# An RWKV-7 recurrence from chunks of 128 tokens to tiles of two 64-token chunks with quarter products

## The chip, the cores and the metric

The kernel runs on one core of a Trainium2 chip. The metric is the device time of one execution in microseconds. The core has TensorE (matmul and, beside it, weight load: PE and PEld in the profile), VectorE (DVE), ScalarE (ACT), GpSimd (POOL) and SyncE (SP), which issues most of the transfers.

## The reference

The first half is a recurrence over 768 tokens for 4 batches of 8 heads with 40 features, in float32. With the state S (40 x 40 for a head) and the token's vectors r, k, v, w, a, b:

```
y_t = r_t S
Sa  = S a_t
S   = S * w_t - Sa b_t^T + v_t k_t^T
```

The outputs y of a token's heads are put together to a row of 320. The second half sends each of the 3072 rows to one of 8 experts by its token id (`id * 2654435761 % 8`) and computes `relu(x @ w1[e]) @ w2[e]`, with w1 of 320 x 1024 and w2 of 1024 x 320.

## The kernel before

The recurrence runs in chunks of 128 tokens of one batch, 24 in all (`chunk`, from line 301). A chunk holds its tokens on the partitions. With P the running product of the decays w inside the chunk, at = a P, bt = b / P and kt = k / P, the chunk needs C from (I + A) C = r1, where A is the strictly lower part of at bt^T (a 128 x 128 block for each head) and r1 comes from the state at the chunk's start and from the values v. From C follow y, and the state after the chunk.

The steps of a chunk stand in this order. VectorE clamps the decays (L312) and takes their least and greatest (L313, L314), TensorE transposes them (L317), VectorE multiplies them up along time with a scan (L321), TensorE turns the result back (L329), VectorE takes the reciprocal (L334), and GpSimd forms at, bt and kt (L335 to L337). `turned` (L264) transposes four 128 x 128 blocks on TensorE and copies the bank on ScalarE. `masked` (L285) multiplies pairs of these for the four heads of one parity and masks the result on VectorE. A head pair lies on partitions 0 to 39 and 64 to 103; `products` (L279) issues four products after each other, all of one parity.

The inverse of I + A is built in seven levels, from blocks of one row to blocks of 64. A level masks A between two blocks on GpSimd (`between`, L351), multiplies it with the inverse so far (x_ps), then again (n_ps), adds on VectorE (L381), and transposes the sum (tm_ps). The last level has 64 x 64 blocks only. After it come r1 (L404 to L408), C (ct_ps, L413), its scores with r (mrc), y (L433 to L438), the state (s_ps, L453 and L454) and its transpose (L463).

Two chunks run at a time, half a chunk apart: each is a generator, and the loop at L471 takes a step of one and a step of the other in turn. That loop stands in a manual schedule: TensorE, VectorE, ScalarE and GpSimd get their instructions in the order in which the program issues them. SyncE's transfers are not bound to it. Each engine runs its own queue in order.

Ahead of the recurrence stands the routing (L122 to L213): each token's place among its expert's slots is counted, and 24 indirect transfers from GpSimd write the token numbers into a list in DRAM (L189), which is read back (L196). The experts' w1 tiles have a pool of their own from the start; the first two experts' w1 are loaded during the recurrence. w2, the gathers of rows (`gather`, L498), `up` (L511) and `down` (L523) follow for expert after expert. At the end a check of the decays decides whether a loop over single tokens runs, and a loop over surplus tiles; neither does in these runs.

Of the kernel before, what the change touches and what calls it, by code (L numbers as in the profile page):

```python
# [36 lines left out]
def kernel(  # L37
# [19 lines left out]
    DP = 64  # L57
    NCH = S // P
    HP = H // 2
    LEVELS = 7  # L60
# [14 lines left out]
    wpool = pool("wpool", 2)  # L75
    ps = pool("ps", 8, space=bass.MemoryType.PSUM)

    def bank(shape, name):
        return ps.tile(shape, F32, tag="ps", name=name)

    # DRAM
# [3 lines left out]
    # masks; s is the partition, t the free index  # L85
# [8 lines left out]
    nupper = const.tile([P, P], F32)  # L94
    nc.vector.tensor_scalar(nupper[:], upper[:], -1.0, None, op0=OP.mult)
    level = []
    for l in range(LEVELS):
        t = const.tile([P, P], F32, name=f"level{l}")
        c2, r2 = (const.tile([P, P], I32, name=f"{n}{l}", tag=n) for n in ("c2", "r2"))
        nc.vector.tensor_scalar(c2[:], col[:], l, None, op0=OP.logical_shift_right)  # L100
        nc.vector.tensor_scalar(r2[:], row[:], l, None, op0=OP.logical_shift_right)
        nc.vector.tensor_tensor(t[:], c2[:], r2[:], op=OP.not_equal)
        nc.vector.tensor_scalar(c2[:], c2[:], 1, None, op0=OP.logical_shift_right)
        nc.vector.tensor_scalar(r2[:], r2[:], 1, None, op0=OP.logical_shift_right)
        e2 = const.tile([P, P], F32, name=f"e2{l}", tag="e2")
        nc.vector.tensor_tensor(e2[:], c2[:], r2[:], op=OP.is_equal)
        nc.vector.tensor_tensor(t[:], t[:], e2[:], op=OP.mult)
        nc.vector.tensor_tensor(t[:], t[:], upper[:], op=OP.mult)
        level.append(t)
# [3 lines left out]
    def over_heads(t):  # L113
        return t[:].unsqueeze(1).to_broadcast([P, HP, P])

    # decays outside LO .. HI are looked for in every chunk
    wmin = route.tile([P, B * NCH], F32)
    wmax = route.tile([P, B * NCH], F32)

# [1 line left out]
    tok_h = dataclasses.replace(moe_token_ids.tensor, shape=list(moe_token_ids.tensor.shape))  # L121
    tok = route.tile([P, TPP, 2], I32)  # L122
    nc.sync.dma_start(tok[:], tok_h.bitcast(I32).rearrange("(p c two) -> p c two", p=P, two=2))
    iota_e = const.tile([P, E], I32)
    nc.gpsimd.iota(iota_e[:], pattern=[[1, E]], base=0, channel_multiplier=0)
    token = const.tile([P, TPP], I32)
    nc.gpsimd.iota(token[:], pattern=[[1, TPP]], base=0, channel_multiplier=TPP)

    eid = route.tile([P, TPP], I32)
    nc.vector.tensor_scalar(eid[:], tok[:, :, 0], E - 1, None, op0=OP.bitwise_and)  # L130
    mine = route.tile([P, E, TPP], F32)
    nc.vector.tensor_tensor(
        mine[:], eid[:].unsqueeze(1).to_broadcast([P, E, TPP]),
        iota_e[:].unsqueeze(2).to_broadcast([P, E, TPP]), op=OP.is_equal)
    mflat = mine[:].rearrange("p e c -> p (e c)")
    tot_ps = bank([P, E * TPP], "tot_ps")
    nc.tensor.matmul(tot_ps[:], lhsT=ones[:], rhs=mflat, start=True, stop=True)
    bef_ps = bank([P, E * TPP], "bef_ps")
    nc.tensor.matmul(bef_ps[:], lhsT=upper[:], rhs=mflat, start=True, stop=True)
    rst = route.tile([P, E, TPP], F32)  # L140
    nc.vector.memset(rst[:], 1.0)
    nc.vector.memset(rst[:, :, 0:1], 0.0)
    cum = route.tile([P, E, TPP], F32)
    cumf = cum[:].rearrange("p e c -> p (e c)")
    nc.vector.tensor_tensor_scan(cumf, rst[:].rearrange("p e c -> p (e c)"), tot_ps[:], 0.0,
                                 op0=OP.mult, op1=OP.add)
    cnt = route.tile([P, E], F32)
# [101 lines left out]
    def flat(t):  # L249
        return t[:].rearrange("p h x -> p (h x)")  # L250
# [424 lines left out]
```

## Time and profile before

| | us |
|---|---|
| median of 3 runs (1681.71 to 1682.19) | 1682.03 |
| span of the profiled execution | 1676.6 |
| TensorE busy | 1510.4 |
| weight loads busy | 1255.9 |
| VectorE busy | 602.3 |
| ScalarE busy | 479.7 |
| GpSimd busy | 534.1 |

The profiled execution is a run of its own; the trace gives its span, from the first to the last instruction, and the time of the runs is a little longer than that span. Busy times are sums over the span and hide that it has stages: a start of some 80 us in which TensorE mostly waits, the recurrence to about 1291 us, and the experts from about 1309 us. A float32 product appears in the trace as two records of a weight load and two of a matmul; a transpose as one of each.

### The profile page before, as it was taken

The page shows a single profiled execution, that of the slowest core. Times are in us where ns is not written, and L with a number is a line of the kernel's source. Part 1 is how long each engine was busy: PE and PEld are TensorE (multiplying, and loading weights), DVE is VectorE, ACT ScalarE, POOL GpSimd, SP SyncE. Part 2 cuts the span into 40 slices and gives each one's busy share as a digit, 9 for nine tenths or more (in the row PEclk, how much of TensorE's full clock was granted, in tenths as well). Part 3 has the DMA queues.
Part 4 walks back from the last instruction along what each step waited for, and adds up shares of the span by engine and source line. Part 5 has one row for each costly group of instructions (what it writes and reads, how often), then busy time and mean ns, then how long its engine had stood idle before and what let it go on. Part 6 is the DMA issues. An engine that isn't in the chain of part 4 may idle for free.

```text
span 1676.6 us, 27809 instructions
## 1 busy us (share of the span) xinstructions
PE 1510.4 (90%) x11622; PEld 1255.9 (75%) x11622; DVE 602.3 (36%) x980; ACT 479.7 (29%) x897; POOL 534.1 (32%) x480
## 2 busy tenths in 40 slices
PE   2399999999999999999999999999997899999996
PEld 1388988988888888888889888899996344444443
DVE  7144444444344444434443444444431111111110
ACT  0143333333333333333333334333331000000000
POOL 5643233443224442234432344423340211111100
PEclk9799999999999999999999999999996799999998
DMA  5111111011101111101111001110001222222200
GB/s 123 13 21 29 29 21 21 17 29 29 29 17 21 21 29 29 23 15 21 29 28 29 17 17 25 29 29 9 5 5 54 79 72 82 91 90 90 83 12 13
DMA packets 172719, 59.58 MB, mean 36 GB/s; under 512 B 156974, under 2 KB 168239, under 8 KB 172592
## 3 DMA queue, kind: packets, MB, share of 16 engines
q1 hardware_dynamic: 168752, 48.58, 13.1%
q0 software_dynamic: 3840, 9.20, 1.7%
q8 instruction: 93, 1.52, 0.4%
q14 instruction: 34, 0.28, 0.1%
HBM read 49.85 MB, written 9.21 MB: 35 GB/s over the span
## 4 chain that ended last, share of the span: by engine, by line
PE 77%; DVE 8%; POOL 6%; issue 5%; DMA 2%; ACT 0%; SPq 0%; POOLq 0%; DVEq 0%; ACTq 0%
PE n_ps L282 13%; PE x_ps L282 13%; PE up_ps L516 12%; PE dn_ps L526 8%; PE tm_ps L268 6%; POOL um L358 4%; PE y_ps L438 3%; PE y_ps L436 2%; PE r_ps L406 2%; PE mrc_ps L282 2%; PE mrv_ps L282 2%; POOL bl L353 2%; DVE um L381 2%; PE ct_ps L413 2%; DVE um L360 2%
## 5 line engine op out<-in xcount | busy, mean ns | idle before, releaser
L353 POOL TENSOR_TENSOR bl<-nat,level 128x512 f32<-128x512 f32 x240 | 309.6, 1318 | 67.3 <-PE x_ps L282 67.3
L282 PE MATMUL n_ps<-um,xm 128*128 128x128 f32 (+1 forms) x2304 | 288.1, 271 | 0.2
L282 PEld LDWEIGHTS n_ps<-um,xm 128*128 128x128 f32 (+1 forms) x2304 | 257.2, 183 | 10.5 <-ACT xm L392 2.4
L282 PE MATMUL x_ps<-tm,bl 128*128 128x128 f32 x1920 | 263.7, 282 | 0.0
L270 ACT COPY tm<-tm_ps 128x512 f32<-128x512 f32 x288 | 169.2, 588 | 329.3 <-PE tm_ps L268 328.1
L381 DVE TENSOR_TENSOR um<-n_ps,um 128x512 f32<-128x512 f32 x240 | 162.8, 687 | 258.3 <-PE n_ps L282 258.3
L282 PEld LDWEIGHTS x_ps<-tm,bl 128*128 128x128 f32 x1920 | 233.5, 193 | 13.8 <-issue 3.9
L268 PE MATMUL tm_ps<-ident,um 128*128 128x128 f32 x1152 | 181.6, 280 | 43.9 <-DVE um L360 26.6
L335 POOL TENSOR_TENSOR at<-al,pr 128x320 f32<-128x320 f32 x24 | 27.9, 1162 | 567.8 <-ACT pr L331 567.8
L516 PE MATMUL up_ps<-xt,w 128*128 128x512 f32 (+1 forms) x384 | 194.5, 637 | 8.7 <-issue 7.5
L374 ACT COPY xm<-x_ps 128x512 f32<-128x512 f32 x240 | 140.7, 586 | 206.1 <-PE x_ps L282 206.1
L268 PEld LDWEIGHTS tm_ps<-ident,um 128*128 128x128 f32 x1152 | 129.8, 143 | 62.1 <-DVE um L381 24.6
L516 PEld LDWEIGHTS up_ps<-xt,w 128*128 128x128 f32 (+1 forms) x384 | 63.4, 191 | 135.5 <-issue 135.5
L526 PE MATMUL dn_ps<-w,ht 128*128 128x320 f32 x512 | 140.0, 434 | 0.0
L526 PEld LDWEIGHTS dn_ps<-w,ht 128*128 128x128 f32 x512 | 96.6, 190 | 45.3 <-issue 6.1
L530 POOL DMA_INDIRECT out_dram<-o,idx_all x32 | 31.7, 990 | 273.0 <-ACT o L529 267.9
L360 DVE TENSOR_TENSOR um<-um,ident 128x512 f32<-128x512 f32 x48 | 82.5, 1718 | 65.0 <-POOL um L358 65.0
L289 DVE TENSOR_TENSOR mrc<-mrc_ps,nupper 128x512 f32<-128x512 f32 x48 | 31.0, 687 | 161.7 <-PE mrc_ps L282 161.7
L358 POOL TENSOR_TENSOR um<-nat,level 128x512 f32<-128x512 f32 x48 | 61.0, 1270 | 80.1 <-DVE nat L289 80.1
L519 DVE TENSOR_SCALAR ht<-up_ps 128x512 f32<-128x512 f32 x32 | 22.2, 692 | 177.4 <-PE up_ps L516 141.5
L438 PE MATMUL y_ps<-bt,mrc 128*128 128x40 f32 x384 | 77.6, 288 | 0.0
L521 ACT ACTIVATE ht<-up_ps 128x512 f32<-128x512 f32 x32 | 19.1, 597 | 199.8 <-PE up_ps L516 199.8
(161 smaller groups left out, 1810.8 us busy)
## 6 DMA issues: line engine op xcount, KB each, us to landing
w<-in_moe_w_dram SPq DMA_DIRECT2D x8, 1280.0 KB, 7.8
w<-in_moe_w_dram SPq DMA_DIRECT2D x8, 1024.0 KB, 5.6
al<-in_a_dram SPq DMA_DIRECT2D x24, 160.0 KB, 2.5
bl<-in_b_dram SPq DMA_DIRECT2D x24, 160.0 KB, 2.6
kl<-in_k_dram SPq DMA_DIRECT2D x24, 160.0 KB, 3.0
w<-in_w_dram SPq DMA_DIRECT2D x24, 160.0 KB, 2.5
v<-in_v_dram SPq DMA_DIRECT2D x24, 160.0 KB, 2.5
r<-in_r_dram SPq DMA_DIRECT2D x24, 160.0 KB, 2.5
```

Source lines behind the costliest of these rows:

```text
L268: nc.tensor.transpose(p[:, hp, :], src, ident[:])
L270: nc.scalar.copy(t[:], p[:])
L282: nc.tensor.matmul(p[out_, hp, cols], lhsT=lhs(hp), rhs=rhs(hp), start=True, stop=True)
L353: nc.gpsimd.tensor_tensor(nxt[par][:], nat[par][:], over_heads(level[l]), op=OP.mult)
L358: nc.gpsimd.tensor_tensor(t[:], nat[par][:], over_heads(level[0]), op=OP.mult)
L360: nc.vector.tensor_tensor(t[:], t[:], over_heads(ident), op=OP.add)
L374: nc.scalar.copy(xm[par][:], x_ps[:])
L381: nc.vector.tensor_tensor(t[:], n_ps[:], um[par][:], op=OP.add)
L406: nc.tensor.matmul(r1_ps[:, h * D:(h + 1) * D], lhsT=mak[par][:, hp, :], rhs=vt[:, h, 0:D], start=first, stop=True, skip_group_check=True)
L438: nc.tensor.matmul(o, lhsT=mrc[par][:, hp, :], rhs=bt[:, h, 0:D], start=False, stop=True, skip_group_check=True)
L516: nc.tensor.matmul(p[:], lhsT=w1[0:m, c, f * P:(f + 1) * P], rhs=xt[0:m, c, 0:n], start=(c == 0), stop=(c == 2))
L526: nc.tensor.matmul(p[:], lhsT=ht[:, f, j * P:(j + 1) * P], rhs=w2[:, f, :], start=(f == 0), stop=(f == FP - 1))
```

## The change

The recurrence is written anew; the experts stay. A tile u is now 64 tokens of two batches, so that the partitions hold 2 x 64 tokens; there are again 24 tiles (12 chunks, two groups of batches). Operands of 40 or 64 partitions are multiplied into 64 output partitions, so that a product takes a quarter of the array: `quarters` walks through the four combinations of head parity (which partitions are read) and batch (which partitions are written), and `scores` writes the two parities to two banks.

The order of all instructions is a plan: each step has a tick and an order, and the sorted plan is issued. A tile has four parts. `tile_a` (at tick u) makes the decay products, at, and b / P (called ba), and sends the blocks of -A that the inverse needs to DRAM. `group_i` inverts the 32-row blocks of four tiles at a time: it reads them from DRAM, one 32 x 32 block on each of the 128 partitions, runs 30 steps of two VectorE instructions, and sends the result back through DRAM. `tile_m` makes the inverse of 64 rows from two blocks of 32. `tile_s` (ten ticks after `tile_a`) loads r, v, k and b again and makes the scores, and `tile_b` makes r1, C, y and the state. The reciprocal of P is kept from `tile_a`.

The check of the decays becomes one comparison of the clamped with the loaded decays. The routing becomes a generator whose steps stand in the plan at ticks 8, 8.5, 9 and so on. The pool of w1 is opened after the recurrence's pools are closed, and the first w1 is loaded there.

The core of the diff:

```diff
-    NCH = S // P
+    C = 64
+    NCH = S // C
+    NG = B // 2
+    NU = NCH * NG
+    BLK = 32
+    GRP = 4
...
-    level = []
...
-    # ---- routing ----
...
+    ps1 = apool("ps1", 2, space=bass.MemoryType.PSUM)
+    ps2 = apool("ps2", 3, space=bass.MemoryType.PSUM)
...
+    HELD = 11
+    LD = 2
...
+    a_dram = [nc.dram_tensor(f"a_blocks{i}", (GRP, 4, H, BLK, BLK), F32) for i in range(NU // GRP)]
+    u_dram = [nc.dram_tensor(f"u_blocks{i}", (GRP, 4, H, BLK, BLK), F32) for i in range(NU // GRP)]
...
+    def quarters(both=True):
+        for hp in range(HP):
+            for p in range(2):
+                for be in range(2):
+                    yield hp, p, be
...
+    def load(dst, src, n, g):
+        for be in range(2):
+            nc.sync.dma_start(
+                dst[half(be), :, 0:D],
+                src[2 * g + be, :, n * C:(n + 1) * C, :].rearrange("h t e -> t h e"))
...
+    def scores(lt, rt, p, co=0):
+        for hp, par, be in quarters():
+            mm(p[half(be), par, co + hp * C:co + (hp + 1) * C],
+               lt[half40(par), hp, half(be)], rt[half40(par), hp, half(be)])
...
+    T1, Q1, T2, Q2, T3, Q3, T4, Q4 = (i / 8 for i in range(8))
...
+    def tile_a(u):
...
+        @at_tick(u - 0.6)
...
+            for nm, src in (("w", w), ("a", a), ("b", b)):
+                x[nm] = work.tile([P, H, D], F32, tag=f"{nm}l", name=f"{nm}l", bufs=LD)
+                load(x[nm], src, n, g)
+        @at_tick(u + T1)
...
+            nc.vector.tensor_scalar(heads(wc), x["w"][:], LO, HI, op0=OP.max, op1=OP.min)
+            p = turn(pairs(wc), "w_ps")
...
+            nc.scalar.copy(dec[:, :, 1:], wt[:, :, 0:C - 1])
...
+        @at_tick(u + T1, 5)
...
+            nc.vector.scalar_tensor_tensor(junk[:], heads(x["wc"]), 0.0, x["w"][:], op0=OP.add,
...
+            nc.vector.tensor_tensor_scan(
...
+            nc.vector.tensor_tensor(pend[:], x["w_ps"][:, :, C - 1], pt[:, :, C - 1], op=OP.mult)
...
+        @at_tick(u + T2, 5)
...
+            nc.gpsimd.tensor_tensor(heads(at), x["a"][:], pr[:], op=OP.mult)
...
+            nc.vector.reciprocal(inv[:], inv[:])
+            nc.gpsimd.tensor_tensor(heads(ba), x["b"][:], inv[:], op=OP.mult)
...
+        @at_tick(u + 1 + Q2, 1)
...
+            scores(x["ba_t"], x["at_t"], p)
...
+            for i in range(2):
+                nc.scalar.mul(na[i][:], pv[:, :, :, i * BLK:(i + 1) * BLK], -1.0)
+            for q in range(4):
+                nc.sync.dma_start(
+                    a_dram[u // GRP][u % GRP, q].rearrange("h s t -> s h t"),
+                    na[q % 2][q * BLK:(q + 1) * BLK].rearrange("s two h t -> s (two h) t"))
+    def group_i(gi):
...
+        t0 = gi * GRP + GRP + 1.0
...
+            nc.sync.dma_start(nb[:], a_dram[gi][:].rearrange("g q h s t -> (g q h) s t"))
...
+            nc.gpsimd.affine_select(ub[:], nb[:], pattern=[[-1, BLK], [1, BLK]], base=0,
...
+        for j in range(1, BLK - 1):
+            @at_tick(t0 + 3.9 * (j - 1) / (BLK - 2), 9)
+            def _(j=j):
+                ub, nb = x["u"], x["n"]
+                m = BLK - 1 - j
+                t = work.tile([P, BLK * BLK // 4], F32, tag="outer", name="outer")
+                tv = t[:, 0:j * m].rearrange("p (c i) -> p c i", c=j)
+                nc.vector.tensor_tensor(tv, ub[:, 0:j, j:j + 1].to_broadcast([P, j, m]),
+                                        nb[:, j, j + 1:].unsqueeze(1).to_broadcast([P, j, m]), op=OP.mult)
+                o = ub[:, 0:j, j + 1:]
+                nc.vector.tensor_tensor(o, o, tv, op=OP.add)
+
...
+            nc.sync.dma_start(u_dram[gi][:].rearrange("g q h s t -> (g q h) s t"), x["u"][:])
+            for i in range(GRP):
+                um = tiles[gi * GRP + i]["um"] = um_r(gi * GRP + i)
+                for q in range(4):
+                    o = (q % 2) * BLK
+                    nc.sync.dma_start(um[q * BLK:(q + 1) * BLK, :, o:o + BLK],
+                                      u_dram[gi][i, q].rearrange("h s t -> s h t"))
...
+    def tile_m(u, t0):
...
+        @at_tick(t0 - 1 + Q4, 2)
...
+            for h in range(H):
+                nc.vector.transpose(t11[:, h, :], um[:, h, 0:BLK])
+            p = bank([P, H, BLK], "x_ps")
+            for hp, par, be in quarters():
+                q = slice(be * C, be * C + BLK)
+                o = slice(be * C + BLK, (be + 1) * C)
+                mm(p[o, hx(par, hp), :], na[q, par, hp, :], t11[q, hx(par, hp), :])
...
+    def tile_s(u, t0):
...
+            for nm, src in (("k", k), ("b2", b)):
+                x[nm] = work.tile([P, H, D], F32, tag=f"{nm}l", name=f"{nm}l", bufs=2)
+                load(x[nm], src, n, g)
...
+        for i, (nm, bufs) in enumerate((("r", 3), ("v", 1), ("kt", 1))):
+            @at_tick(t0 - 1 + (T1, T2, T3)[i], 2)
+            def _(nm=nm, bufs=bufs):
+                x[nm + "_t"] = turned(pairs(x[nm]), nm + "_t", bufs)
...
+            p = two_banks("m_ps")
+            scores(x["kt_t"], x["at_t"], p)
+            scores(x["v_t"], x["r_t"], p, HP * C)
...
+            nc.vector.tensor_tensor(t[:], p[:].rearrange("p two (h t) -> p (two h) t", t=C),
+                                    after[:].unsqueeze(1).to_broadcast([P, 4 * HP, C]), op=OP.mult)
...
+    def from_state(p, lt, s):
...
+    def tile_b(u, t0):
...
+            @at_tick(t0 - 1 + Q4, 1)
...
+                from_state(p, x["at_t"], st)
...
+        @at_tick(t0 + Q1, 0)
...
+            for hp, par, be in straight_then_crossed():
+                mm(p[half(be), par, hp * D:(hp + 1) * D], mak(x, par, hp)[half(be)],
+                   head(x["v"], par, hp)[half(be)], start=first and hp == 0)
...
+            nc.scalar.copy(by_pair(r1), heads_of(p))
...
+        @at_tick(t0 + Q2, 0)
...
+                mm(p[half(par), be, hp * C:(hp + 1) * C], head64(x["r1"], par, hp)[half(be)],
+                   x["um"][half(be), hx(par, hp), :])
...
+            @at_tick(t0 + T3, 0)
...
+                p = turn([ct[:, hp, :, :] for hp in range(HP)], "nc_ps")
...
+        @at_tick(t0 + Q3, 1)
...
+            @at_tick(t0 + Q3, 2)
...
+                for src, rhs, begin in ((x["kt"], x["v"], True), (x["bt"], x["nct"], False)):
+                    for hp, par, be in quarters():
+                        mm(p[half(par), be, hp * D:(hp + 1) * D], head64(src, par, hp)[half(be)],
+                           head(rhs, par, hp)[half(be)], start=begin and hp == 0, stop=not begin)
...
+        @at_tick(t0 + Q4, 3)
...
+                mm(o, mrv(x, par, hp)[half(be)], head(x["kt"], par, hp)[half(be)],
+                   start=first and hp == 0, stop=False)
+                mm(o, x["mrc"][half(be), par, hp, :], head(x["bt"], par, hp)[half(be)], start=False)
...
+            nc.vector.tensor_tensor(by_pair(xs), heads_of(p), by_pair(x["pr"]), op=OP.mult)
...
+            @at_tick(t0 + Q4, 6)
...
+    LAG = 10
+    for u in range(NU):
+        tile_a(u)
+        tile_s(u, u + LAG)
+        tile_m(u, u + LAG)
+        tile_b(u, u + LAG)
+    for gi in range(NU // GRP):
+        group_i(gi)
...
+    steps = routing()
+    for i in range(12 + TPP):
+        at_tick(8 + 0.5 * i, 7)(lambda: next(steps, None))
...
+        for *_, f in sorted(plan, key=lambda e: e[:3]):
+            f()
     a_ctx.close()
+    wpool = pool("wpool", 2)
+    w1s[0] = load_w1(moe_w1[0], "w1_0")
```

## Rows read from the trace of the kernel before

**Rows 1.** Busy time by stretch; columns: us, PE, PEld, DVE, ACT, POOL, PEclk, DMA share, GB/s

```profile
40.00:80.00 40.00, 10.64 (x67) 9.62 (x68) 5.00 (x7) 3.52 (x6) 25.63 (x25) 0.81 0.20 14
...
700.00:1000.00 300.00, 283.16 (x2633) 264.18 (x2632) 131.54 (x189) 111.04 (x209) 109.08 (x90) 1.00 0.13 23
...
1280.00:1320.00 40.00, 26.09 (x83) 16.42 (x83) 6.02 (x17) 0.60 (x1) 9.55 (x10) 0.53 0.37 111
```

**Rows 2.** The chain of waits in order of time; columns: start us, us, what

```profile
56.64 9.13 DMA slot_tokens<-token,key_i
...
1205.79 1.95 PE x_ps L282 x16
...
1253.46 1.95 PE x_ps L282 x16
...
1291.99 6.59 DMA x_rows<-xs
...
1308.86 28.05 PE up_ps L516 x48
```

**Rows 3.** Groups of the inverse on TensorE; columns: line, shapes, count | busy us, mean ns

```profile
L282 PE MATMUL x_ps<-tm,bl 128*128 128x128 f32 x1920 | 263.7, 282 | 0.0
...
L268 PE MATMUL tm_ps<-ident,um 128*128 128x128 f32 x1152 | 181.6, 280 | 43.9 <-DVE um L360 26.6 <-DVE um L381 17.2
```

**Rows 4.** Order of time, weight loads; columns: start us, us, engine, line, shapes, count

```profile
1003.98 0.20 PEld L453 LDWEIGHTS s_ps<-v,kt 128*64 128x64 f32 x4
...
1004.79 0.22 PEld L454 LDWEIGHTS s_ps<-nct,bt 128*64 128x64 f32 x4
...
1012.12 0.47 PEld L268 LDWEIGHTS tm_ps<-ident,um 128*128 128x128 f32 x4
...
1012.55 0.47 PEld L268 LDWEIGHTS v_t_ps<-ident,v 128*128 128x128 f32 x4
...
1034.54 0.97 PEld L282 LDWEIGHTS n_ps<-um,xm 128*128 128x128 f32 x8
...
1035.63 0.54 PEld L282 LDWEIGHTS x_ps<-tm,nat 64*64 64x64 f32 x8
...
1036.24 0.86 PEld L282 LDWEIGHTS n_ps<-um,xm 128*128 128x128 f32 x7
```

**Rows 5.** Order of time, matmuls of the two parities

```profile
62.72 0.27 PE L282 MATMUL mak_ps<-at_t,kt_t 40*128 40x128 f32 x1
...
62.72 0.27 PE L282 MATMUL nat_ps<-at_t,bt_t 40*128 40x128 f32 x1
```

**Rows 6.** Groups by shape on VectorE, ScalarE and GpSimd

```profile
L180 DVE TENSOR_TENSOR slot<-slot,rank 128x24 f32<-128x24 f32 x1 | 0.2, 164 | 0.0
...
L441 DVE TENSOR_TENSOR xs<-y_ps,pr 128x320 f32<-128x320 f32 x24 | 11.8, 492 | 89.5 <-PE y_ps L438 89.5
...
L321 DVE TENSOR_TENSOR_SCAN pt<-dec,restart 128x516 f32<-128x516 f32 x24 | 29.3, 1222 | 0.0
...
L334 DVE RECIPROCAL inv<-inv 128x320 f32<-128x320 f32 x24 | 51.7, 2153 | 0.8
...
L360 DVE TENSOR_TENSOR um<-um,ident 128x512 f32<-128x512 f32 x48 | 82.5, 1718 | 65.0 <-POOL um L358 65.0
...
L130 DVE TENSOR_SCALAR eid<-tok 128x24 int32<-128x24 int32 x1 | 9.4, 9382 | 1.1 <-DMA tok<-in_moe_token_ids_dram 1.1
...
L270 ACT COPY tm<-tm_ps 128x512 f32<-128x512 f32 x288 | 169.2, 588 | 329.3 <-PE tm_ps L268 328.1 <-ACT r_t L270 0.2
...
L335 POOL TENSOR_TENSOR at<-al,pr 128x320 f32<-128x320 f32 x24 | 27.9, 1162 | 567.8 <-ACT pr L331 567.8
```

**Rows 7.** The transfers: a queue with its share, issues with median us to landing

```profile
q1 hardware_dynamic: 168752, 48.58, 13.1%
...
w<-in_moe_w_dram SPq DMA_DIRECT2D x8, 1024.0 KB, 5.6
...
al<-in_a_dram SPq DMA_DIRECT2D x24, 160.0 KB, 2.5
```

More of the change, by code (lines that the diff above doesn't have):

```diff
@@ L125 @@
[L125 to L144, printed above, removed]
@@ new lines, in bank, with two_banks, pairs, by_pair @@
+    def bank(shape, name):
+        return ps1.tile(shape, F32, tag="ps1", name=name)
+    def two_banks(name):
+        return ps2.tile([P, 2, 512], F32, tag="ps2", name=name)
+    def pairs(t):
+        return [t[:, 2 * hp:2 * hp + 2, :].rearrange("p two x -> p (two x)") for hp in range(HP)]
+    def by_pair(t):
+        return heads(t).rearrange("p (hp two) e -> p two hp e", two=2)
+    def half(i):
+        return slice(i * C, (i + 1) * C)
+    def half40(i):
+        return slice(i * C, i * C + D)
@@ L324, in chunk @@
         yield
[L325 removed]
+        nc.vector.tensor_tensor(cumf, cumf, sums[:, 0, :], op=OP.subtract)
+        nc.vector.tensor_tensor(cumf, cumf, sums[:, 1, :], op=OP.add)
         yield
[L327 to L332 removed]
@@ L355, in chunk @@
[L355 to L361 removed]
+        for c in range(TPP):
+            st = nc.gpsimd.indirect_dma_start(
+                out=slot_dram[:, None],
+                out_offset=bass.IndirectOffsetOnAxis(ap=key_i[:, c:c + 1], axis=0),
+                in_=token[:, c:c + 1], in_offset=None, bounds_check=NT * P - 1, oob_is_err=False)
+            tc.declare_no_dep(st.ins, group="slots", reason="distinct slots")
+            tc.add_to_no_dep_group("slots", st.ins)
@@ L397, in chunk @@
-        yield
-        r1_ps = bank([P, DM], "r1_ps")
-        for h in range(H):
-            hp, par = divmod(h, 2)
-            if par == 0 and not first:
-                nc.tensor.matmul(r1_ps[:, h * D:(h + 2) * D], lhsT=at_t[:, hp, :], rhs=pair(st, hp),
-                                 start=True, stop=False, skip_group_check=True)
-            nc.tensor.matmul(r1_ps[:, h * D:(h + 1) * D], lhsT=mak[par][:, hp, :], rhs=vt[:, h, 0:D],
-                             start=first, stop=True, skip_group_check=True)
@@ L408, in chunk @@
-        nc.scalar.copy(heads(r1), by_head(r1_ps))
-        yield
-        ct_ps = bank([P, HP, P], "ct_ps")
-        for h in range(H):
-            hp, par = divmod(h, 2)
-            nc.tensor.matmul(ct_ps[par * DP:(par + 1) * DP, hp, :], lhsT=r1[:, h, :], rhs=um[par][:, hp, :],
-                             start=True, stop=True)
-        ct = two.tile([P, HP, P], F32, tag="ct", name="ct")
-        nc.scalar.copy(ct[:], ct_ps[:])
-        yield
-        mrc = [masked(par, ct, r_t, nupper, one, "mrc") for par in range(2)]
@@ L440, in chunk @@
-        xs = two.tile([P, H, D], F32, tag="xs", name="xs")
-        nc.vector.tensor_tensor(xs[:], by_head(y_ps), pr[:], op=OP.mult)
-        t0 = bi * S + ci * P
-        nc.sync.dma_start(x_rows[t0:t0 + P, :], xs[:].rearrange("p h e -> p (h e)"))
-        yield
-        if last:
-            return
-        s_ps = bank([P, HP, D], "s_ps")
-        for h in range(H):
-            hp, par = divmod(h, 2)
-            o = s_ps[par * DP:(par + 1) * DP, hp, :]
-            nc.tensor.matmul(o, lhsT=kt[:, h, :], rhs=vt[:, h, 0:D], start=True, stop=False)
-            nc.tensor.matmul(o, lhsT=bt[:, h, :], rhs=nct[:, h, :], start=False, stop=True)
```

559 lines of the change are left out of this document (291 added, 268 removed).

## The prediction

> **What bounds the kernel now.** I read the busy shares by stretch first, then the chain of waits in order of time, then the groups of instructions by shape, and last the order of time itself around the operations that the change uses.
>
> Between 700 and 1000 us TensorE is busy 283 of 300 us at full clock, the other engines between 109 and 132 us [rows 1]: in the recurrence the bound is TensorE. The chain of waits agrees: the same x_ps group returns after 47.7 us (1205.79 to 1253.46), one chunk of 128 tokens [rows 2]. Of this the larger part is the inverse: the x_ps products of 128 x 128 have 263.7 us of TensorE's busy time, the n_ps products are as many again, and the transposes between levels (tm_ps) have 181.6 us [rows 3]: together some 700 of about 1230 us. Ahead of it stands a start in which TensorE waits: in 40 to 80 us it is busy 10.6 us [rows 1], because the 24 indirect DMAs of the routing sit on GpSimd in front of the first chunk's at, bt and kt, and the last of them lands at 65.8 us [rows 2]. The recurrence ends with the x_rows write at 1292.0 us; the experts' first product starts at 1308.9 us [rows 2]. From the last y product (1291.4 us, 0.6 ahead of that write) to the end of the span are 385 us, which the change leaves alone but for one load.
>
> The profiled span is 1676.6 us; the median of the runs is 1682.0, so I add 5.4 us to a span.
>
> **TensorE's price of a quarter product.** The change works in 24 tiles u (64 tokens of two batches), laid out in ticks, stage b ten ticks behind stage a. Ticks 0 to 9 hold stage a alone, 10 to 23 everything, 24 to 33 all but a. I count from the diff what a full tick gives TensorE: 32 transposes of 128 x 128 in groups of four (w, p, at, ba, r, v, kt, nct), and 240 small products: scores 16 + 32 + 16, x and u 32, r1 32, c 16, state 32, y 48, sd 16.
>
> Four transposes follow the next four after 0.43 us (1012.12 to 1012.55) [rows 4]: 8 x 0.43 = 3.5 us. The nearest row to a quarter product is s_ps (64 columns of weights, 40 moving): a float32 product is two records, and its 32 records start between 1003.98 and 1004.87 us (the last line's end, 1005.01, less one load of 0.14), 29 ns each, while they alternate between the two column halves [rows 4]. In one position the 64 x 64 x_ps starts a record every (0.54 - 0.13) / 7 = 58 ns [rows 4]. So two positions run side by side at twice the pace. Two row halves do so too: records of mak (upper rows) and nat (lower rows) start in the same 62.72 us [rows 5]. Four positions at once no row shows. Bounds for a product: 30 ns (four side by side), 58 ns (two), 117 ns (none). I take 58, the row itself: 240 x 0.058 = 13.9 us.
>
> The Trainium skill, "TensorE: Matmul & The Clock Gate", section "Wait — 56ns, not 53.3ns?", says that matmul starts never come closer than about 25 ns however short they are. By it 480 records need at least 12 us a tick, and the sum would be about 2 us a tick lower; the 29 ns row agrees, and by this rule the four-fold pace of the fast rival does not come.
>
> Changing the shape costs too: after the eight n_ps loads the next would be due at 1035.43 (pace 0.111), the 64 x 64 load comes at 1035.63; on the way back 0.15 us are lost [rows 4]. Nine changes a tick by 0.17: 1.5 us. TensorE's sum for a full tick: 3.5 + 13.9 + 1.5 = 18.9 us.
>
> **VectorE, ScalarE, GpSimd in a full tick.** 24 elements take 0.164, 320 take 0.492 us [rows 6]: 0.137 us and 1.11 ns an element. The inverse of four tiles is 60 operations, j(31-j) elements for j = 1 to 30 twice, 9,920 in all: 8.2 + 11.0 = 19.2 us, 4.8 a tick. Stage a: clamp, compare and the product for 1/P 0.49 each, scan 1.22, reciprocal 2.15, one small one: 5.0. Masks on 1024 and 512 elements 1.27 + 0.70, state 0.98, y 0.49: 3.4. Eight 32-column transposes, not shown before, at the price of 32 elements: 1.4 (half to double of it: 0.7 to 2.8). Sum 14.6 us, below TensorE, but not far: where VectorE works from SBUF beside GpSimd, 512 elements took 1.72 us instead of 0.7 [rows 6], and GpSimd has four products a tick at up to 1.16 us [rows 6]; at worst these 4.6 us come on top: 19 us. ScalarE: seven copies of 512 at 0.59 [rows 6] and nine smaller ones, about 8 us, hidden. GpSimd loses its 240 level products; at 4 us and 2.6 us of indirect DMAs in some ticks it is hidden.
>
> **What is not hidden in a tick.** The eight transposes of t11 stand on VectorE behind the 1.27 us mask of mm, which waits for the last m_ps product; TensorE has only the 16 r1 products (0.9 us) to do until x_ps needs t11: 0.2 + 1.3 + 1.4 - 0.9 = 2.0 us less one shape change already counted, 1.8. Transposes have two banks, so the third group of four waits for a 0.59 us copy: about 0.8 in two places. Full tick: 18.9 + 2.6 = 21.5 us. A last-stage tick has 16 transposes and 16 products less (1.7 + 0.9) and loses their cover, so c waits for r1's copy and nct for ct's (0.3 + 0.9), while the bank waits mostly go: 18 us.
>
> **The ten first ticks.** A chain from engine to engine: clamp 0.5, transpose 0.9 (0.6 at full clock, twice that at the lower level), copy 0.59, scan 1.22, transpose 0.9, copy 0.45, product 0.49, reciprocal 2.15, hand-overs 0.8: 8 us, five times. From tick 5 the inverse adds 4.8, of which some 2 hide while TensorE and ScalarE have the chain: 11 us, five times. 95 us.
>
> **Routing, start, experts.** The start loses the seven level masks and the routing: 8 us until the first clamp (a load lands in 2.5 us [rows 7], then short memsets). The bitwise instruction of the routing held VectorE 9.4 us once [rows 6]; why the trace does not say, so 0 to 9.4 in its new place at tick 8, where VectorE bounds: I take 9. The w1 load of expert 0 now comes only when the recurrence has given its memory back: 1024 KB land in 5.6 us [rows 7], beside the 17 us of write and gathers, but on the same queue as the x_rows write, with 5 MB of w1 and w2 near it. 0 to 28 us (four times 1280 KB at that rate), I take 8, about one expert's load.
>
> **Sum.** Start 8, first ticks 95, bitwise 9, 14 x 21.5 = 301, 10 x 18 = 180: 593 us to the last y, against 1291 before. Then 385 + 8. Span 986, time 986 + 5.4 = 992 us. Late next is the y, state and score block of each tick on TensorE, with VectorE a few us behind it.
>
> **The rivals.**
> Four positions side by side. For it: column halves and row halves each overlap [rows 4, 5]. TensorE's tick is 3.5 + 7.1 + 1.5 = 12.1, and VectorE becomes the bound: 14.6 and half of GpSimd's time, 16.5; last ticks 13. 8 + 95 + 9 + 231 + 130 = 473, time 871. Against: 29 ns for a weight load and a product may be the engine's own pace of issue.
>
> VectorE and the hand-overs decide in stacked waits (contention in full, t11 at its upper price, masks late for the bank that the next product wants): tick 27, last ticks 23. 8 + 95 + 9 + 378 + 230 = 720, time 1118. For it: the 1.72 us row. Against: GpSimd is idle most of a tick.
>
> The quarters do not overlap, so the change does not do what it says: 117 ns, TensorE 33.1, tick 35, last ticks 31: time 1310. Against: rows 4 and 5.
>
> TensorE falls to the lower of its levels (1.2 GHz) throughout. For it: 0.53 of the clock at 1280 to 1320 us, after the gaps of the last chunk [rows 1]. All its terms double: tick 40, last ticks 34, time 1410. Against: 1.00 wherever it is kept busy, as the full ticks keep it.
>
> Slower than before: the transfers bound a tick. Seven loads of 1024 pieces of 160 bytes, 2048 pieces of 128 bytes through DRAM for the inverse and some 270 others make 9,500 packets a tick, where a chunk now has 6,300 in 47.7 us. The queue took 13.1% of 16 engines for 168,752 packets, 20.8 ns each [rows 7]: 12.3 us a tick, hidden. It decides above 21.5 us (36 ns a packet), and makes the kernel slower above 48.8 us, 82 ns; at 90 ns the time is 112 + 24 x 53.4 + 393 + 5 = 1792. Against: four times the price in the row, though writes of 128 bytes to DRAM are not in it.
> The Trainium skill, "DMA: Bandwidth & Descriptors", section "Specifications", asks for 512 bytes for full rate, with a read-modify-write below that. If the 1024 written pieces of a tick cost double by it, a tick has 1.3 us more of transfers; no run here shows such writes.
>
> **How the numbers follow.** Forecast (940 to 1080) 0.50; four positions (830 to 940) 0.17; stacked waits (1080 to 1230) 0.17; no overlap 0.08; low clock 0.04; transfers 0.03; within 0.2%, what a measurement here can tell from no change, 0.01. The range, 865 to 1230, leaves out the lower third of the second case and, above, the three dear ones: about 0.2. All cases but transfers and the 0.01 are faster: 0.96.
>
> **What would show it.** Right: TensorE busy about nine tenths in the full ticks, 21 to 22 us between two tiles' y writes, 18 near the end, some 110 us until the first tick with products of stage b, waits for t11 ahead of x_ps. s_ps and score records 29 ns apart: 15 speaks for the first rival, 58 for the third. Wrong: VectorE busier than TensorE, SyncE's loads ended by waits on transfers, a granted clock near 0.5 in full ticks, or over 20 us between the last y write and the first product of the experts.

## The result, and the profile after

The changed kernel takes 1123.28 us (median of 4 runs, 1118.59 to 1126.07), the one before 1681.87 beside it: a ratio of 0.668, interval 0.6655 to 0.6697. The forecast was 992, the range 865 to 1230. The direction and the range hold; the size is 131 us short. The profiled execution took 1123.06 us, with a span of 1121.2.

The busy shares by stretch of the changed kernel; its columns are those of [rows 1]. The first line lies in the full ticks, the second in the last ones:

```profile
300.00:400.00 100.00, 84.37 (x1950) 75.84 (x1950) 57.60 (x130) 27.83 (x60) 24.85 (x26) 0.64 0.42 67
...
660.00:700.00 40.00, 37.18 (x817) 33.83 (x818) 7.83 (x25) 8.73 (x18) 1.79 (x3) 0.50 0.13 25
```

TensorE is still the busiest engine by far; VectorE, at 58%, is not the bound. New is the clock. In the recurrence before it was 1.00 [rows 1]; here it is 0.64 in the full ticks, and 0.50, the lower of the two levels, in the last ones, where TensorE is busy 37.18 of 40 us.

The chain of waits in order of time, as in [rows 2]; one y group for each tile:

```profile
149.80 3.59 PE y_ps L194 x64
...
511.06 3.59 PE y_ps L194 x64
...
677.68 3.59 PE y_ps L194 x64
700.64 3.59 PE y_ps L194 x64
...
732.10 3.65 PE y_ps L194 x62
...
753.68 28.16 PE up_ps L698 x48
```

From the first y (149.80) to the fourteenth (511.06) are 13 ticks of 27.8 us; 21.5 were predicted. From there to the last (732.10) are ten of 22.1 on average, 23.0 for the steady one shown; 18 were predicted. The last y ends at 735.75 instead of 593.

One full tick in order of time on TensorE, as in [rows 4], but matmuls; behind a group stands the idle time ahead of it and what ended it:

```profile
351.85 1.92 PE L194 MATMUL u_ps<-um,xi 32*64 32x32 f32 x32
353.70 1.93 PE L194 MATMUL r_ps<-v,mm 64*64 64x40 f32 x32
355.56 1.11 PE L199 MATMUL p_ps<-ident,pt 128*128 128x128 f32 x4
356.47 1.06 PE L199 MATMUL v_t_ps<-ident,v 128*128 128x128 f32 x4
357.46 1.13 PE L194 MATMUL c_ps<-um,r 64*64 64x64 f32 x32
358.37 1.08 PE L194 MATMUL a_ps<-at_t,ba_t 40*64 40x64 f32 x32
...
361.37 0.68 PE L194 MATMUL y_ps<-sd,r_t 40*64 40x40 f32 x32
361.86 0.67 PE L194 MATMUL rc_ps<-r_t,ct 40*64 40x64 f32 x32
...
364.71 0.69 PE L194 MATMUL m_ps<-at_t,kt_t 40*64 40x64 f32 x32 [1.12 <-DVE mrc L482]
...
368.97 1.33 PE L194 MATMUL x_ps<-t,na 32*32 32x32 f32 x32 [2.57 <-DVE t L355]
```

Take the distance from one start to the next. The 32 records of u take 1.85 us, 58 ns each; the 32 of c take 0.91 us, 28 each; those of the y part from the state, at 361.37, take 0.49 us, 15 each. Two things are mixed in this. The products of u, of r1 from v, of x, of sd and 64 records of y use two positions of the array, the diagonal ones (a half of the rows with the same half of the columns); c, a, m, rc, s and the products with the state use all four. And the granted clock by slices of the same trace changes in between:

```profile
357.00:361.00 4.00, 3.91 (x77) 3.22 (x76) 3.72 (x4) 2.71 (x7) 2.14 (x3) 0.64 0.06 12
361.00:365.00 4.00, 2.88 (x150) 2.63 (x152) 3.83 (x8) 0.90 (x2) 3.54 (x4) 1.00 0.45 70
365.00:369.00 4.00, 1.43 (x94) 1.31 (x86) 3.45 (x9) 0.00 (x0) 0.26 (x1) 0.71 0.45 40
```

At the upper level (2.4 GHz) a four-position record takes 15 ns, at the lower (1.2 GHz) 28; a two-position record takes 58 at the lower, 29 at the upper, as experiment 1 shows. A tick has 144 products in four positions and 96 in two. With two records to a product, eight groups of transposes at 0.43 us [rows 4] and 1.5 us of shape changes, TensorE would need 3.5 + 4.3 + 5.6 + 1.5 = 14.9 us at the upper level, less than the 18.9 of the prediction; at the lower, with 0.95 for four transposes, 7.6 + 8.1 + 11.1 = 26.8 before any shape change. The tick shown (341.37 to 370.30) has 23.6 us busy and 5.3 idle.

### The profile page after: what moved, and what is told of

It is laid out like the page before. It is cut to its first block, busy times and chain, and to the rows that moved or that the text cites. A ratio compares the mean times of both kernels' runs of the same rounds, so it can differ in the third digit from the quotient of the medians.

```text
span 1121.2 us, 29486 instructions
## 1 busy us (share of the span) xinstructions
PE 920.9 (82%) x12958; PEld 682.6 (61%) x12958; DVE 416.6 (37%) x1003; ACT 213.5 (19%) x446; POOL 194.4 (17%) x223
## 3 DMA queue, kind: packets, MB, share of 16 engines
q1 hardware_dynamic: 250736, 65.12, 29.8%
## 4 chain that ended last, share of the span: by engine, by line
PE 68%; DVE 15%; issue 4%; SPq 4%; DMA 3%; ACT 3%; POOL 1%; POOLq 0%; DVEq 0%; ACTq 0%
PE up_ps L698 17%; PE dn_ps L708 12%; PE y_ps L194 8%; PE r_ps L194 4%; PE u_ps L194 4%; DVE ub L330 3%; DVE outer L327 3%; PE sd_ps L194 3%; DVE inv L279 3%; SPq L339 3%; PE m_ps L194 2%; PE r_t_ps L199 2%; PE w_ps L199 2%; DVE mm L407 2%; PE x_ps L194 2%
## 5 line engine op out<-in xcount | busy, mean ns | idle before, releaser
L701 DVE TENSOR_SCALAR ht<-up_ps 128x512 f32<-128x512 f32 x32 | 22.1, 691 | 177.5 <-PE up_ps L698 141.6
L194 PE MATMUL y_ps<-kt,mm 64*64 64x40 f32 x768 | 83.3, 306 | 0.1
L330 DVE TENSOR_TENSOR ub<-ub,outer 128x30 f32<-128x30 f32 (+9 forms) x180 | 80.8, 449 | 6.6
L194 PE MATMUL y_ps<-bt,mrc 64*64 64x40 f32 x768 | 82.4, 304 | 0.8 <-DVE mrc L482 0.8
L327 DVE TENSOR_TENSOR outer<-ub,nb 128x30 f32<-128x30 f32 (+9 forms) x180 | 71.4, 397 | 8.0 <-POOL ub L316 4.5
L194 PE MATMUL x_ps<-t,na 32*32 32x32 f32 x768 | 30.1, 237 | 50.7 <-DVE t L355 46.1
L194 PEld LDWEIGHTS y_ps<-bt,mrc 64*64 64x64 f32 x768 | 68.9, 223 | 0.9 <-issue 0.9
L194 PEld LDWEIGHTS y_ps<-kt,mm 64*64 64x64 f32 x768 | 68.0, 211 | 1.7 <-issue 0.2
L199 PE MATMUL w_ps<-ident,wc 128*128 128x128 f32 x96 | 26.3, 429 | 49.1 <-DVE wc L247 39.4
L194 PEld LDWEIGHTS x_ps<-t,na 32*32 32x32 f32 x768 | 23.9, 146 | 57.1 <-DVE t L355 42.2
L279 DVE RECIPROCAL inv<-inv 128x320 f32<-128x320 f32 x24 | 51.7, 2153 | 0.8
```

The source lines that it names most:

```text
L194: nc.tensor.matmul(out_, lhsT=lhsT, rhs=rhs, start=start, stop=stop, skip_group_check=True)
L199: nc.tensor.transpose(p[:, hp, :], src, ident[:])
L279: nc.vector.reciprocal(inv[:], inv[:])
L327: nc.vector.tensor_tensor(tv, ub[:, 0:j, j:j + 1].to_broadcast([P, j, m]), nb[:, j, j + 1:].unsqueeze(1).to_broadcast([P, j, m]), op=OP.mult)
L330: nc.vector.tensor_tensor(o, o, tv, op=OP.add)
L701: nc.vector.tensor_scalar(ht[:, f, 0:n], p[:], 0.0, None, op0=OP.max)
```

## The experiments

`warm` in the diffs is one bf16 product of 128 x 128 by up to 512 columns into the bank just taken, which the real products then overwrite. The diffs are shortened. Ratios are to the kernel before, with their intervals.

**1 to 3. Work that is only there for the clock.** One full-size product at each bank taken:

```diff
     def bank(shape, name):
-        return ps1.tile(shape, F32, tag="ps1", name=name)
+        t = ps1.tile(shape, F32, tag="ps1", name=name)
+        warm(t, 128, 1)      # e2: warm(t, 128, 2); e3: warm(t, 64, 2)
+        return t
```

> The changed kernel with one extra product of the whole array (128 rows, 128 columns, bf16, up to 512 moving columns, its result overwritten) at each of the some 18 PSUM allocations of a tick; nothing else differs. Extra work: about 8500 columns a tick, 3.5 us at full clock, 7 us at half. Theory A (the granted clock of 0.5 to 0.65 in the ticks is what the prediction missed, and quarter products on their own do not hold the upper level): the clock in 300 to 500 us rises from 0.62 to over 0.85, a full tick goes from 27.5 to about 22 us although TensorE has more to do, and the time from 1123 to about 1000 us. Theory B (VectorE and the hand-overs bound the tick, the low clock only fills waits): the clock may rise, but the time stays within 1110 to 1140. Theory C (the clock does not depend on what TensorE is given): clock 0.62, a tick longer by up to 7 us, time about 1200 to 1270.

> As the run with one extra product, with two at each allocation: 7 us more for TensorE a tick at full clock, 14 at half. Theory A: clock over 0.9 in all full ticks and in the last ones, a full tick about 24 us, the time about 1030 us: the clock gains little more and the extra work costs 3.5 us a tick more. Theory B: about 1123 to 1160. Theory C: about 1350.

> As the run with two extra products at each allocation, but each on 64 rows and 64 columns of the array: as many instructions and moving columns, a quarter of the array. If the time in which TensorE is busy is what holds the clock, this does the same as the run with two whole-array products: clock over 0.9, about 1030 us. If the part of the array that works counts (theory A in its narrow form), the clock stays below 0.75 and the extra columns cost 8 to 14 us a tick: 1250 to 1400 us.

Measured: e1 1113.26 us, 0.6627 (0.657 to 0.6684); e2 1155.11, 0.6876 (0.6786 to 0.6966); e3 1420.99, 0.8459 (0.84 to 0.8518). The busy shares of the full ticks, one product (first fence), then two on a quarter of the array (second):

```profile
300.00:400.00 100.00, 86.77 (x2022) 71.37 (x2034) 58.71 (x134) 29.08 (x62) 24.87 (x26) 0.84 0.45 72
...
412.00:416.00 4.00, 3.85 (x82) 3.00 (x83) 2.68 (x3) 2.74 (x7) 1.18 (x1) 1.00 0.11 22
...
420.00:424.00 4.00, 2.93 (x127) 2.12 (x119) 3.02 (x9) 0.00 (x0) 0.03 (x1) 1.00 0.38 38
```

```profile
300.00:400.00 100.00, 96.77 (x1293) 67.86 (x1286) 39.46 (x95) 17.22 (x37) 11.87 (x12) 0.50 0.28 42
```

With 18 full-size products a tick the clock rises from 0.64 to 0.84 and stays at 1.00 for at least 12 us of a tick. The order of time at the end of that stretch shows y's two-position records at both levels: four records in 0.115 us, 29 ns each, and from 426.69 on in 0.20 and more, after 1.6 us of y without a gap and 1.18 us of idle time ahead of x:

```profile
424.11 1.00 PE L211 MATMUL x_ps<-t,na 32*32 32x32 f32 x32 [1.18 <-DVE t L372]
425.04 0.32 PE L211 MATMUL y_ps<-kt,mm 64*64 64x40 f32 x4
...
426.23 0.31 PE L211 MATMUL y_ps<-kt,mm 64*64 64x40 f32 x4
426.35 0.31 PE L211 MATMUL y_ps<-bt,mrc 64*64 64x40 f32 x4
...
426.69 0.44 PE L211 MATMUL y_ps<-kt,mm 64*64 64x40 f32 x4
426.89 0.45 PE L211 MATMUL y_ps<-bt,mrc 64*64 64x40 f32 x4
```

Some 430 more products left the kernel no slower, so what they cost the clock gave back. The clock came as theory A had it, the time did not: 1113 us instead of about 1000, and 26.8 us instead of 22 from one y to the next in the full ticks (156.28 to 504.95 us, 13 ticks). In e2 the second product raised the clock no further (0.83 in the same stretch) and cost 42 us; its 1030 was missed as well. e3 has the instructions of e2 on a quarter of the array and came out a little above its 1250 to 1400. In it TensorE is busy 97% and the clock is 0.50 for the whole stretch: with products on a quarter of the array, and some transposes, a high busy share did not bring the upper level. The Trainium skill, "TensorE: Matmul & The Clock Gate", "Part 1: The HAM clock gate", says that the lower level is the default and that a busy TensorE is released from it; e3's trace does not agree.

**4. Is VectorE the bound?** 29 of the 30 steps of the inverse are left out:

```diff
-        for j in range(1, BLK - 1):
+        for j in range(1, 2):
```

> The changed kernel with 1 of the 30 VectorE steps of each group's inverse; 29 steps are left out, so the blocks' inverses are not computed. VectorE has about 25 us less in four ticks. Theory A: only the waits for t11, the masks and the first ticks go, the clock stays under 0.7: full ticks 27.5 to about 25, first ticks 3 us shorter each from the fifth on, time about 1060 to 1080. Theory B (VectorE bounds): full ticks fall to about 21 us, time 980 to 1000.

Measured: 1087.10 us, 0.6471 (0.643 to 0.6513). This is short of both theories. VectorE falls from 58 to 33% in the full ticks, the start of the first y comes 15.7 us earlier, and the full ticks shrink by 1.3 us, to 26.5:

```profile
300.00:400.00 100.00, 82.11 (x2001) 72.83 (x1999) 33.07 (x74) 28.29 (x61) 21.94 (x23) 0.70 0.43 69
...
134.09 2.43 PE y_ps L194 x64
```

The rival of stacked waits, whose band (1080 to 1230) holds the measured time, is near it by luck. Some of its waits are in the trace (46.1 us for t11, 12.5 us for the mask mrc), but it had VectorE decide in the full ticks, where the steps of the inverse are worth 1.3 us, and it had nothing of the lower clock.

**5. The waits.** The t11 transposes go ahead of mm's mask on VectorE, and the 16 um reads of a group, which SyncE issued in one lump, go one tile a tick:

```diff
-        @at_tick(t0 - 1 + Q4, 2)
+        @at_tick(t0 - 1 + Q3, 2.5)
+            ... t11's transposes
+        @at_tick(t0 - 1 + Q4, 2)
             ... x_ps
@@ group_i
-            for i in range(GRP):
+        for i in range(GRP):
+            @at_tick(t0 + 3.92 + 0.9 * i)
```

> The changed kernel with two moves in the plan and nothing more or less to do: the eight t11 transposes of VectorE ahead of the mask of mm instead of behind it, and the 16 reads of the inverted blocks spread over four ticks instead of issued at once. If the waits are worth what the trace shows (x_ps waited 46 us for t11; the reads hold SyncE's queue for 8 to 13 us in every fourth tick, and the next decay load stands behind them, some 3 us five times): about 1123 - 46 - 15 = 1062 us. If TensorE at its lower clock is the bound and the waits move elsewhere: 1100 to 1123 us. The granted clock stays at 0.6 to 0.7 either way.

What asked for it, in the changed kernel: its waits (total us, times, longest), and SyncE's queue in order of time:

```profile
PE x_ps L194 <- DVE t L355: 46.1, 22, 5.5
PE w_ps L199 <- DVE wc L247: 39.4, 8, 6.9
```

```profile
220.74 13.09 SPq L339 DMA_DIRECT2D um<-u_blocks  x16
...
236.31 0.66 SPq L210 DMA_DIRECT2D wl<-in_w_dram  x1
```

Measured: 1082.46 us, 0.6428 (0.6393 to 0.6463), 41 us under the changed kernel. From the first y to the 14th a tick is 26.7 us, from there to the last 20.3, against 27.8 and 22.1. This lies between the two expectations. The wait for t11 falls from 46.1 to 5.0 us, and the last wait for w ends at 122 us. The end shows plainest what remains: TensorE is busy 97%, and it is still at the lower level:

```profile
500.00:600.00 100.00, 97.18 (x2188) 90.08 (x2188) 44.17 (x132) 22.19 (x47) 8.62 (x11) 0.50 0.37 62
600.00:640.00 40.00, 38.59 (x795) 35.59 (x794) 6.08 (x20) 9.46 (x20) 3.36 (x4) 0.50 0.30 60
```

The two moves were not run apart; e9, below, bears on what the wait for w is worth.

**6 to 8. Cheaper ways to the clock, and the loads.** In e6 and e7 the full-size products stand inside the two-position stretches (u, r1, y, sd), 13 and 23 a tick; both have the moves of e8. e9 is the changed kernel with the loads of w, a and b a tick earlier.

```diff
+                if i % 8 == 0:                     # e7: i % 4
+                    warm(p[:, H:, :])              # unused columns of the same bank
                 mm(p[half(be), h, :], xi[q, h, :], um[q, h, BLK:C])
```

> The two moves, and one extra product of the whole array (bf16, 192 to 512 columns, into columns of the bank that nobody reads) after each eight quarter products of u, r1, y and sd, at the allocation of r1's and y's banks and of x's: 13 a tick, none in the other blocks. These blocks (two positions of the array at a time) ran at half pace after the clock fell in y. Theory A (clock): it stays over 0.9 from y to r1, the y block takes 2.5 us instead of 3.6, a full tick 21 us, a last one 17, the time 960 to 1000 us. If eight quarter products between two wide ones are still too many: clock 0.7 to 0.8 and about 1050 us. Theory C: no gain over the run with the two moves alone, 3 us a tick more.

> As the run before with an extra product after each four quarter products instead of eight: 23 a tick. If the clock needs this much, it is over 0.9 here and lower there, and this is the faster of the two, 980 us; if the wider spacing is enough, this is slower by ten products of 0.3 us a tick: about 60 us more than the run before.

```diff
-    LD = 2
+    LD = 3
-        @at_tick(u - 0.6)
+        @at_tick(u - 1.6)
```

> The changed kernel with three buffers instead of two for the loads of w, a and b, asked for one tick earlier; nothing else. If the first ticks and some later ones wait for the landing of w (in the chain w's landing stands with 2.3 to 2.7 us at 39, 90, 124, 236 and 458 us): about 12 to 20 us less, 1105 us, the first y block 12 us earlier than 149.8. If the queue of SyncE is what is late, and not the buffer: no change.

Measured: e6 1216.10, 0.7223 (0.7198 to 0.7248); e7 1326.53, 0.7879 (0.7845 to 0.7913); e9 1125.16, 0.67 (0.6682 to 0.6718). Both expectations for the clock were missed. With 23 a tick (e7):

```profile
300.00:400.00 100.00, 94.39 (x1323) 68.06 (x1322) 36.56 (x84) 20.28 (x43) 14.76 (x16) 0.57 0.29 49
```

The clock of the full ticks is no higher than without them, and they cost 134 and 244 us, more than the 0.3 us each that was expected: in y of e7 eight records with one such product take 1.00 us instead of 0.43. Each stands alone between quarter products, with a change of shape before and behind it. So it is not the number of full-size products either: 18 a tick spread over all banks raise the clock, 23 in the y, r1, u and sd stretches do not (they are smaller, 192 to 512 columns each). What the chip asks for stays open. The early loads (e9) leave the time as it was, but not because w still came late: the waits for w fall from 39.4 us (8 times) to 23.1 (5 times), with none left in 200 to 500 us, and the first y starts at 145.5 instead of 149.8. A full tick takes 28.4 us instead of 27.8, and in 200 to 500 us waits with nothing named grow from 4.2 to 10.7 us. So the lateness of w, taken away by itself, brought nothing.

**9 to 11. Five places, four positions, both gains.** f1 is e8 with one full-size product at sd, w, ba, r and u. f2 is e8 with y and r1 issued over four positions; f3 is e1 and e8 together.

```diff
+        if name in ('sd_ps', 'w_ps', 'ba_t_ps', 'r_t_ps', 'u_ps'):     # f1
+            warm(t, 128, 1)
@@ f2
-            for hp, par, be in straight_then_crossed():
-                mm(o, mrv(x, par, hp)[half(be)], ...)
+            for hp, par, be in quarters():
+                mm(o, mrv(x, par, hp)[half(par)], ...)
```

> The kernel with the moved transposes and spread reads (1082) plus one bf16 product of 128x128 on the whole array at five places a tick only: where the banks of sd, w, ba, r and u are taken, the stretch in which the granted clock was 0.50 or was about to rise. Five of them cost about 5 x 0.32 = 1.6 us a tick, some 38 us over 24 ticks, at a clock that doesn't move. Theory A (the full-size products beside sd, w, ba and r bring the clock up some 6 us earlier in each tick, as the run with 18 a tick showed): 3 us saved for 1.6 paid, 24 x -1.4 = -34, about 1050. Theory B (only a steady mix over the whole tick does it): 1082 + 38 = 1120, granted clock of the ticks as before, 0.57 to 0.64.

> The same base (1082), with the products of y and r1 issued over four positions of the array in turn instead of two: the row half follows the parity of the head instead of the batch, so that for half of the combinations the other batch's tokens are multiplied; count, shape and data volume stay. Theory A (the two-position order is the price: 58 ns a product at half clock against 27): y's 32 products among 64 records take 1.75 instead of 3.6 us, r1 (32) 0.9 instead of 1.8, so 24 x -2.7 = -65: about 1017, at the clock of before. Theory B (the two-position stretches are also what lets the clock fall): the clock stays up for longer, full ticks of 22 us or less, about 960. Theory C (the ticks wait for something else): y and r1 shorten and waits take their place, over 1060.

> The 18 full-size products a tick (alone: 1113 against 1123, -10) together with the moved transposes and spread reads (alone: 1082, -41). Theory A (they act on different times, clock and waits): 1123 - 51 = 1072. Theory B (with the waits gone the products lie wholly on TensorE's path, 18 x 0.32 = 5.8 us a tick at a clock that gains less): 1100 to 1130.

Measured: f1 1094.54, 0.6469 (0.6437 to 0.6502); f2 1047.24, 0.6231 (0.621 to 0.6252); f3 1077.04, 0.6417 (0.6379 to 0.6455). Five products raised the clock (0.60 to 0.72 in 300 to 400 us) but returned only some 26 of the 38 us that they were reckoned to cost, a rough figure, since the intervals of f1 and e8 overlap. In the full ticks they paid for themselves (26.6 us against 26.7); the loss is in the first ticks (the first y 6.6 us later) and in the last ones (23.1 us against 22.0), where the clock stayed at 0.50 (600 to 640 us). f3 cannot be told from e8 by its time, but its ticks are others. A full tick takes 28.8 us instead of 26.7, at a clock of 0.67 to 0.81 in 200 to 500 us; a last one takes 16.8 instead of 20.3, at 0.90, though it has 13 more products to do. So in this trace the last ticks get the upper level, and there it pays; full-size products in these alone were not tried:

```profile
300.00:400.00 100.00, 91.37 (x1982) 72.22 (x1980) 57.20 (x131) 28.57 (x60) 24.90 (x26) 0.81 0.42 66
...
600.00:640.00 40.00, 39.12 (x1047) 31.40 (x1050) 10.29 (x36) 11.26 (x24) 3.37 (x4) 0.90 0.36 71
```

f2 confirms the price of the two-position order; half of its y and r1 products multiply the other batch's tokens, so it shows a price and is no kernel to use. y's groups start at half the distance, with the clock at 0.50:

```profile
420.88 0.47 PE L194 MATMUL y_ps<-kt,mm 64*64 64x40 f32 x8
421.12 0.45 PE L194 MATMUL y_ps<-bt,mrc 64*64 64x40 f32 x8
421.33 0.46 PE L194 MATMUL y_ps<-kt,mm 64*64 64x40 f32 x8
```

27 ns a record instead of 58. The steady last ticks go from 21.97 to 19.48 us, the 2.5 us that the paces of y and r1 give. The full ticks gain only 1.2, while a stall grows that none of the theories had: TensorE stands still with nothing named that it waits for. In the stretch of quick records of f2:

```profile
412.06 0.76 PE L194 MATMUL s_ps<-nct,bt 64*64 64x40 f32 x10
413.22 0.29 PE L194 MATMUL s_ps<-nct,bt 64*64 64x40 f32 x3 [0.41 <-issue]
413.94 0.33 PE L194 MATMUL s_ps<-nct,bt 64*64 64x40 f32 x5 [0.43 <-issue]
414.69 0.45 PE L194 MATMUL s_ps<-nct,bt 64*64 64x40 f32 x13 [0.42 <-issue]
...
418.30 0.22 PE L194 MATMUL r_ps<-st,at_t 40*64 40x40 f32 x1 [2.08 <-issue]
```

In 260 to 490 us such gaps are 30.0 us in f2, 11.9 in e8 and 3.3 in the changed kernel, where waits stand in their place.

**12. Do these gaps come from the transfers?** f2 without the way of the blocks through memory; the inverse works on zeros:

```diff
-                nc.sync.dma_start(a_dram..., na...)
-            nc.sync.dma_start(nb[:], a_dram...)
-            nc.sync.dma_start(u_dram..., x["u"][:])
-                    nc.sync.dma_start(um..., u_dram...)
```

> The four-position kernel (1047) without the way of the blocks through memory: the writes of na, the read of nb, the write of ub and the reads of um are left out (98 thousand of the 250 thousand packets of the SyncE queue), and the inverse runs on zeros, with all its VectorE instructions. In the four-position kernel TensorE stood still for 29 us of 260 to 490 us for nothing that the profile names, in gaps of 0.4 to 3.2 us. Theory A (these gaps come with the load on the DMA engines): they fall below 12 us in such a stretch, which is 14 x 1.8 = 25 us, and with the first ticks free of the 4.6 us read and of SyncE's lump the time is about 1010. Theory B (they don't come from the transfers): 25 us or more remain, only the first ticks gain, 1030 to 1040. The granted clock is expected as before, 0.6 to 0.64, in either.

Measured: 1041.14 us, 0.6201 (0.6183 to 0.6219). The SyncE queue has 196,784 packets instead of 250,736: 54 thousand fewer, not the 98 of the expectation. The gaps in 260 to 490 us remain, 27.4 us in all; the lines are waits of TensorE there:

```profile
PE sd_ps L196 <- issue: 8.2, 5, 3.9
PE s_ps L196 <- issue: 6.8, 18, 0.7
PE y_ps L196 <- issue: 5.7, 4, 3.1
```

So theory B: they don't come from these transfers, a fifth of the packets; the rest was not tried. Most stand in the stretches in which records start 15 ns apart, or some microseconds behind them; that TensorE's own supply of instructions runs dry there would fit, but was not tried.

## Why the prediction was right in direction and short in size

**The bound.** TensorE bounds the full and the last ticks, as predicted; VectorE (58%, and experiment 4) does not.

**The price of a product: the step that failed.** The prediction multiplied 240 products by 58 ns at the clock of the recurrence before, and set the rival of the low clock aside at 0.04 with "1.00 wherever it is kept busy, as the full ticks keep it". That is what failed: kept busy at 84 to 97%, with quarter products, TensorE was granted 0.50 to 0.64. The rival's own 1410 us did not come, because the second half of the step was wrong in the other direction. Products side by side in four positions run at 15 ns a record at the upper level, 30 ns a product instead of 58, which I had given 0.17 as a rival. The Trainium skill, "TensorE: Matmul & The Clock Gate", section "Wait — 56ns, not 53.3ns?", that the prediction quoted with its floor of about 25 ns between starts, does not hold here: 32 records in 0.49 us. The products of a last tick show both errors: at the rows' paces of the lower level, 4 x 0.95 + 128 x 0.057 + 96 x 0.116 = 22.2 us, where the steady tick takes 23.0; at the upper level the same rows give 1.7 + 3.8 + 5.6 = 11.1, and the prediction had 16.3 with the shape changes (18.9 - 1.7 - 0.9), 18 with the waits. That the range holds is thus in part luck: one error is too dear and the other too cheap.

**Waits in a tick.** The wait for t11 was in the right place and of the right size: 46.1 us in 22 ticks is 2.1, predicted 1.8. The bank wait (r_t behind the ba copy, 0.68 us) too. Two were missing: the mask mrc (1.12 us in the tick shown), and SyncE. The 16 reads of a group held its queue for 7.8 to 13.8 us, and behind three of the first four such groups w's load came late, with 4.1 to 4.5 us of waiting. By e9 that lateness brings nothing back when it alone goes. The prediction had priced the packets, and rightly (29.8% for 250,736 packets is 21.3 ns each, against 20.8 [rows 7]), but not SyncE's own time to issue them.

**The first ticks.** The first tick with stage b begins at 127.2 us instead of 112. The first steps take 7.7 us where nothing waits, as reckoned (8); from the sixth on it is 15.4 us on average (50.0 to 127.2 us) instead of 11. Without the steps of the inverse (experiment 4) it is still 13.1 (50.1 to 115.6 us). So the steps are worth 11.6 us of these five ticks, less than the 15 that the prediction added for them; what it put at nothing is the loads: in the chain of experiment 4 from 50 to 135 us SyncE's issuing has 32% and landings some 18%. In the last of the five SyncE issues the 16 reads first and w's load behind them, and the tick waits for w, with the steps (first two lines) and without them (third line, experiment 4):

```profile
115.01 7.80 SPq L339 DMA_DIRECT2D um<-u_blocks  x16
127.23 1.09 PE L199 MATMUL w_ps<-ident,wc 128*128 128x128 f32 x4 [4.50 <-DVE wc L247]
...
115.62 1.08 PE L199 MATMUL w_ps<-ident,wc 128*128 128x128 f32 x4 [7.81 <-DVE wc L247]
```

The steps themselves are slower than their sizes say, as the groups of the changed kernel show, in the columns of [rows 6]:

```profile
L330 DVE TENSOR_TENSOR ub<-ub,outer 128x228 f32<-128x228 f32 x12 | 10.2, 851 | 0.4
...
L330 DVE TENSOR_TENSOR ub<-ub,outer 128x240 f32<-128x240 f32 x12 | 5.4, 453 | 0.4
```

All steps take 152 us, 25.4 a group instead of 19.2. Whether GpSimd's work beside them is the cause was not tried.

**Costs that did not come.** The bitwise instruction took 0.17 us in its new place, not 9, and w1's load left the time from the last y to the experts as it was (17.9 us), 0 instead of 8:

```profile
L558 DVE TENSOR_SCALAR eid<-tok 128x24 int32<-128x24 int32 x1 | 0.2, 168 | 0.0
```

**The sum.** Start and first ticks +15 (with the 9 not paid), 14 full ticks at 27.8 +88, ten last at 22.1 +41, w1 -8, what lies around the span 2 instead of 5 us: 992 + 133 = 1125, measured 1123. By an estimate from the rows the clock alone is worth more than the miss: at the upper level they give TensorE 14.9 us a tick, below the 18.9 of the forecast. No run held the full ticks there; the last ticks of f3, at 0.90 and with 13 more products, took 16.8 us, below the 18 of the forecast.

The fastest versions that keep the kernel's work are e8 (1082) and f3 (1077), not to be told apart; both beat the changed kernel by about 4%.

## What to carry to other kernels

A clock read under full-size products may not be carried over to products on a part of the array: price them at both levels, and let the range reach to the lower one. Look at which positions of the array follow each other, since products over two diagonal positions have half the pace of products over all four. And a group of small transfers costs twice, on the engines that move it and in the queue that issues it: spread it, or what stands behind it in that queue is late. Whether that costs time is another question: in e9 it did not.

## What was not expected of the hardware

Four 64 x 64 positions in turn start a record every 15 ns at the upper level and 28 at the lower; two diagonal ones every 29 and 58. With such products and some transposes TensorE stays at 1.2 GHz at a busy share of 97% (e3, e8), and full-size products raised it when they stood at the banks (18 a tick, 0.82 to 0.84 in e1; five a tick, 0.65 to 0.72 in f1), not when they stood inside the two-position groups (23 a tick, 0.57 to 0.64 in e7). All these are of 200 to 500 us, where e8, without them, has 0.60 to 0.64. In and behind stretches of 15 ns records TensorE stands still for 0.4 to 3.9 us at a time with no wait shown, some 3 us a tick in f2 and f4. In the first 120 us of the trace the clock reads 1.00 while four transposes take 1.06 to 1.12 us, as in the ticks where it reads 0.50: there the pace is the better witness.
